# Attention into a two-layer MLP on one core: the first two attention units in steps of one pair of heads, and the first four MLP units over 512 tokens at once

## The chip, the core and the metric

The program runs on one core of a Trainium2 chip. The core has a matrix engine (TensorE, PE in the profile, with its weight loads as PEld), three engines for element-wise work (VectorE as DVE, ScalarE as ACT, GpSimd as POOL), and DMA queues that SyncE (SP) fills. The metric is the device time of one execution in microseconds; the median of the runs is quoted.

## What is computed

```python
# q, k, v: (2, 8, 768, 64);  x: (1536, 512);  d_ff = 2048, two MLP layers
k_sum = k.reshape(B, H, nb, 32, D).max(axis=3)       # 24 summary keys
v_sum = v.reshape(B, H, nb, 32, D).mean(axis=3)
scores_l = where(|i-j| < 16, q @ k.T / 8, -1e9)      # local window
scores_s = q @ k_sum.T / 8 + log(32)
a = softmax(concat(scores_l, scores_s))              # divided by sum + 1e-9
x = a @ concat(v, v_sum)
h = x @ moe_w_in                                     # layer 1
g = (a0 + a1*h + a2*h^2 + a3*h^3) / (1 + |b0||h| + |b1|h^2 + 1e-6)
x = g @ moe_w_out
h = x @ moe2_w_in;  out = (h * cos(h)) @ moe2_w_out  # layer 2
```

The weights arrive as 64-bit floats and are unpacked on the chip. Every MLP product is done in three matmuls on high and low parts (high by high, high by low, low by high), so that one MLP step has three matmuls where a plain one has one.

## The kernel before

Attention is cut into 12 units of 128 tokens with all 8 heads, which are held as 4 pairs (`NP`). A unit `u` goes through three functions. `attn_a` copies the keys of two windows of 96 tokens and the 24 summary keys into `kw`, makes 16 score matmuls into two PSUM tiles `sp`, then for each of its 8 (pair, head) slices one masked minimum on DVE (line 664) and one exponential on ACT (line 668), and at its end the normalisation (lines 672 to 683, the last step on POOL or DVE). `attn_b` transposes the normalised scores (8 matmuls into `ptp`, copies into `pt`). `attn_c` multiplies with the values (16 pairs of matmuls into `avp`) and stores the result as a high and a low part, `xH` and `xL`. Keys of the first batch are made by `k_pair`: one pair of heads at a time, in two DMAs, two groups of transposes (`ktp`), two copies and two maxima. `q_tile` transposes queries into `qT`; `v_mean0` makes the summary values.

The MLP is cut into units of one block `f` of 128 hidden features and one tile `T` of 512 tokens. `mlp_h` makes `h` from 12 matmuls, `ew1` works out the rational function on ACT, DVE and POOL (some ten instructions, then `split_g` into `gh` and `gl`), and `mlp_o` accumulates 12 matmuls into four PSUM tiles `acc`. `mlp_o` follows `mlp_h` three units later. `conv` unpacks the weights of one `f` (two matrices, each three DVE steps and a split into high and low). Only the first tile (layer 1, group 0, `T` 0) is cut in two halves of 256 tokens: line 992 gives it 8 units of 256 tokens, so the first four can begin when attention units 0 and 1 are done.

The order on every engine comes from a planner (class `Plan`). The functions above record operations with the engines that could run each one and an assumed cost; `fill` lists the attention steps, and the loop at lines 1080 to 1088 lays them between the MLP units so that an MLP unit comes after the attention units it needs (`pos_need`). The planner then works out latest times backwards from the end and places operations forwards by those times and by how soon an engine is free. Tile pools limit it: `ps` has four PSUM buffers that `sp`, `h` and some of the transposes share, `gh` and `gl` have three each, `raw` has three and the windows `kw` two. Each engine runs its list strictly in that order.

```python
992    subs = [(0, 256), (256, 256)] if (l, g, T) == (0, 0, 0) else [(0, TT)]
1046       pos_need.append(need[(TT * un.T + un.c + un.n) // 128 - 1])
```

Of the kernel before, what the change touches and what calls it, by code (L numbers as in the profile page):

```python
# [9 lines left out]
F32 = mybir.dt.float32  # L10
# [276 lines left out]
SPT = 1.2  # L287
# [3 lines left out]
def kernel(  # L291
# [322 lines left out]
    pr_t, pt_t = {}, {}  # L614
# [4 lines left out]
    def attn_a(u):  # L619
# [4 lines left out]
        sps = [psum([128, NP, KW], f"sp{hh}") for hh in range(2)]  # L624
        kks = {kr["k", i, y] for w in ws for i in range(w // 128, (w + WK - 1) // 128 + 1)
               for y in range(NP)}
        kw = kws[u % NKW]
        if t < NKW:
            P.op([("P", Shared(0.6)), ("A", act(192))], [kr[x] for x in kr.subs if x[0] == "s"], [kw["s"]],
                 lambda e: cp(e, kw.t[:, :, :, WK:KW],  # L630
                              ks().unsqueeze(2).to_broadcast([128, NP, 2, NB])))

        def windows(e):
            if ws[1] - ws[0] == 64:
                x = kk()[:, :, ws[0]:ws[0] + 128].rearrange("p n (a s) -> p n a s", a=2)
                x = bass.AP(x.tensor, x.offset, [x.ap[0], x.ap[1], x.ap[2], [1, WK]])
                cp(e, kw.t[:, :, :, 0:WK], x)
            else:
                for half in range(2):
                    cp(e, kw.t[:, :, half, 0:WK], kk()[:, :, ws[half]:ws[half] + WK])  # L640

        n = 768
        P.op([("P", Shared(1.2)), ("A", act(n)), ("V", dvef(n))], sorted(kks, key=id), [kw["w"]], windows)

        def mm(e):
            for pr in range(NP):
                for half in range(2):
                    for hh in range(2):
                        p0, c0 = 64 * hh, 64 * half
                        nc.tensor.matmul(out=sps[hh].t[c0:c0 + 64, pr, :],  # L650
                                         lhsT=qt.t[p0:p0 + 64, pr, c0:c0 + 64],
                                         rhs=kw.t[p0:p0 + 64, pr, half, :], start=True, stop=True)

        P.op([("T", SPT)], [qt, kw["s"], kw["w"]], sps, mm)
        su = new("sm", [128, 2, NP], F32, "su", 3)
        mn = new("sm", [128, 2, NP], F32, "mn", 3)
        m = masks[offs]
        scs = []
        for hh in range(2):
            sc = new("at", [128, NP, KW], F32, "sc", 4)  # L660
            sp = sps[hh]
            for pr in range(NP):
                P.op([("V", 0.19)], [sp], [sc[pr], mn[hh, pr]],
# [6 lines left out]
                         bias=mn.t[:, hh, pr:pr + 1], accum_out=su.t[:, hh, pr:pr + 1]))  # L670
            sus = [su[hh, pr] for pr in range(NP)]
# [12 lines left out]
            scs.append((sc, ss))  # L684
        pr_t[u] = scs
        P.now += SPT
# [324 lines left out]
    def add_a(u):  # L1011
        b, t = divmod(u, UPB)
        if u == 0:
            for i in range(NP):
                fill.append((k_pair, i, 30.0))
        elif t == 0:
            for i in range(6):
                fill.append((k_tile, i, LEADK))
        fill.append((q_tile, u, 30.0 if u < 2 else 8.0))
        fill.append((attn_a, u))  # L1020
        if t == 0:
            fill.append((v_mean1, LEADK) if b else (v_mean0, 24.0))
# [102 lines left out]
```

## Time and profile before

| | |
|---|---|
| median of 3 runs | 619.33 us (617.93 to 620.05) |
| profiled execution | 618.5 us, its span 616.8 us |
| PE busy | 595.5 us, 97% of the span |
| DVE, ACT, POOL busy | 477.8, 396.4, 413.7 us |
| granted clock of PE, mean | 0.994 |

The 618.5 us are the whole profiled execution, the span is the stretch from its first to its last instruction; 1.7 us lie outside it. A busy share of PE includes the drain of a matmul, so PE's rate is better read from the start of one matmul to the start of the next. The idle time of PE and what ended it is read from the list of waits, and its place in the program from the timeline.

### The profile page before, as it was taken

Reading aid. Unit: us, or ns where it says so; the run is one execution under the profiler, and the core shown is the slowest. Engines: PE = TensorE matmul, PEld = TensorE weight load, DVE = VectorE, ACT = ScalarE, POOL = GpSimd, SP = SyncE. Lnnn points to the kernel's source line nnn. Section 1 sums busy time; section 2 is a strip of 40 time slices with the busy share of each in tenths; the row PEclk is TensorE's granted clock in tenths of the full one; section 3 lists DMA queues with packets and bytes.
Section 4 is the critical chain, followed back from the end, with each engine's and each line's share of the span. In section 5 each row is a group of like instructions: output and inputs, shape, how many; then the busy total and the mean of one; then the engine's idle time right before and its main releaser. Section 6 shows DMA issues by size and latency. Waiting matters only on the chain.

```text
span 616.8 us, 9933 instructions
## 1 busy us (share of the span) xinstructions
PE 595.5 (97%) x3516; PEld 489.9 (79%) x3516; DVE 477.8 (77%) x919; ACT 396.4 (64%) x842; POOL 413.7 (67%) x409
## 2 busy tenths in 40 slices
PE   8778997999999999999999999999999999999997
PEld 7467876787888888888888878888888888888886
DVE  3999887758899989999999899569656875773541
ACT  5988799668767666786677656455455446544553
POOL 4487984657987878789868777568446754574332
PEclk9989999899999999999999999999999999999999
DMA  8986963100221222112122124213201330000112
GB/s 247 261 231 161 251 181 103 27 1 35 69 69 35 69 69 69 55 59 94 34 73 77 57 71 136 67 41 102 98 28 41 104 102 2 34 1 1 69 51 86
DMA packets 68714, 51.80 MB, mean 84 GB/s; under 512 B 37288, under 2 KB 62888, under 8 KB 68664
## 3 DMA queue, kind: packets, MB, share of 16 engines
q1 hardware_dynamic: 68376, 51.16, 28.0%
q8 instruction: 28, 0.46, 0.3%
q14 instruction: 22, 0.18, 0.1%
q10 hardware_dynamic: 288, 0.00, 0.0%
HBM read 47.71 MB, written 3.15 MB: 82 GB/s over the span
## 4 chain that ended last, share of the span: by engine, by line
PE 61%; DVE 20%; ACT 9%; POOL 4%; issue 3%; DMA 3%; SPq 0%; DVEq 0%; ACTq 0%; POOLq 0%
PE acc L943 29%; PE h L820 28%; ACT sc L668 2%; DVE te L868 2%; DVE tu L876 2%; DVE h L879 2%; DVE te L866 2%; DVE te L882 2%; DVE f L784 2%; DVE f L788 2%; DVE f L780 2%; ACT h L874 1%; PE avp L742 1%; POOL tu L864 1%; DMA big<-in_v_dram 1%
## 5 line engine op out<-in xcount | busy, mean ns | idle before, releaser
L820 PE MATMUL h<-xH,w 128*128 128x512 f32 (+1 forms) x544 | 172.8, 380 | 3.3 <-ACT pt L360 2.2
L839 POOL TENSOR_TENSOR gl<-te,gh 128x512 fp32r<-128x512 f32 (+1 forms) x100 | 135.0, 1350 | 7.4 <-ACT gh L360 0.9
L362 POOL TENSOR_SCALAR gh<-te 128x512 fp32r<-128x512 f32 (+1 forms) x84 | 59.3, 706 | 100.9 <-DVE te L906 80.9
L943 PE MATMUL acc<-gh,w 128*128 128x512 f32 (+1 forms) x416 | 123.5, 380 | 1.3 <-POOL gh L362 1.3
L820 PEld LDWEIGHTS h<-xH,w 128*128 128x128 f32 x544 | 100.9, 189 | 23.4 <-ACT pt L360 2.7
L943 PE MATMUL acc<-w,gh 128*128 128x512 f32 x384 | 118.4, 389 | 0.4 <-DVE xL L965 0.4
L820 PE MATMUL h<-xL,w 128*128 128x512 f32 (+1 forms) x272 | 103.0, 379 | 0.1
L898 DVE SCALAR_TENSOR_TENSOR h<-tu,h 128x512 f32<-128x512 int32 x96 | 66.4, 691 | 36.0 <-ACT te L360 34.9
L820 PE MATMUL h<-big,w 128*128 128x512 f32 x384 | 92.1, 389 | 0.9 <-DVE te L882 0.9
L943 PEld LDWEIGHTS acc<-gh,w 128*128 128x128 f32 x416 | 76.2, 190 | 16.6 <-POOL gh L362 1.5
L794 POOL TENSOR_TENSOR w<-f,w 128x512 fp32r<-128x512 f32 x62 | 84.2, 1360 | 6.2 <-ACT w L360 3.9
L820 PEld LDWEIGHTS h<-big,w 128*128 128x128 f32 x384 | 72.0, 188 | 16.3 <-DVE te L882 1.4
L943 PEld LDWEIGHTS acc<-w,gh 128*128 128x128 f32 x384 | 72.0, 188 | 15.8 <-DVE xL L965 0.9
L864 POOL TENSOR_TENSOR tu<-tu,tf 128x512 f32<-128x512 f32 (+1 forms) x52 | 67.1, 1291 | 19.6 <-ACT tf L856 19.5
L943 PE MATMUL acc<-gl,w 128*128 128x512 f32 (+1 forms) x208 | 78.3, 377 | 0.2 <-POOL gl L839 0.2
L943 PE MATMUL acc<-w,gl 128*128 128x512 f32 x192 | 74.7, 389 | 0.0
L901 ACT ACTIVATE h<-h 128x512 f32<-128x512 f32 x48 | 27.9, 582 | 60.4 <-DVE h L898 60.4
L906 DVE TENSOR_TENSOR te<-te,h 128x512 f32<-128x512 f32 x48 | 32.9, 685 | 35.1 <-ACT h L903 34.9
L820 PEld LDWEIGHTS h<-xL,w 128*128 128x128 f32 x272 | 51.3, 189 | 9.4 <-DVE xL L753 0.3
L893 ACT ACTIVATE tu<-h 128x512 int32<-128x512 f32 x48 | 28.7, 598 | 45.7 <-PE h L820 45.7
L784 DVE SCALAR_TENSOR_TENSOR f<-raw,f 128x512 int32<-128x512 int32 x64 | 56.1, 877 | 0.5
L788 DVE SCALAR_TENSOR_TENSOR f<-raw,f 128x512 int32<-128x512 int32 x64 | 56.0, 875 | 0.6
(100 smaller groups left out, 974.7 us busy)
## 6 DMA issues: line engine op xcount, KB each, us to landing
raw<-in_moe_w_in_dram SPq DMA_DIRECT2D x32, 512.0 KB, 3.7
raw<-in_moe_w_out_dram SPq DMA_DIRECT2D x32, 512.0 KB, 3.3
vw<-in_v_dram SPq DMA_DIRECT2D x24, 192.0 KB, 4.7
qk<-in_q_dram SPq DMA_DIRECT2D x10, 256.0 KB, 3.8
out_dram<-part SPq DMA_DIRECT2D x8, 256.0 KB, 2.0
part<-in_k_dram SPq DMA_DIRECT2D x8, 192.0 KB, 4.6
big<-in_v_dram SPq DMA_DIRECT2D x3, 512.0 KB
qk<-in_k_dram SPq DMA_DIRECT2D x6, 256.0 KB, 3.3
```

The lines of the kernel that those rows point to most:

```text
L362: nc.gpsimd.tensor_scalar(out=o, in0=i, scalar1=1.0, scalar2=1.0, op0=ALU.mult, op1=ALU.mult)
L784: lambda e, lohi=lohi, ft=ft: nc.vector.scalar_tensor_tensor(out=ft.t.bitcast(I32), in0=lohi()[1], scalar=-0x40000000, in1=ft.t.bitcast(I3 ...
L788: lambda e, lohi=lohi, ft=ft: nc.vector.scalar_tensor_tensor(out=ft.t.bitcast(I32), in0=lohi()[0], scalar=29, in1=ft.t.bitcast(I32), op0=A ...
L794: lambda e, ft=ft, w=w: E[e].tensor_tensor(out=w.t[:, 1, :], in0=ft.t, in1=w.t[:, 0, :].bitcast(F32), op=ALU.subtract),
L820: nc.tensor.matmul(out=h.t[:, 0:n], lhsT=lt, rhs=rt[:, kk, cs], start=(k0 == 0 and i == 0), stop=(k0 == 2 and i == 5))
L839: lambda e: E[e].tensor_tensor(out=un.gl.t[:, 0:n], in0=g.t[:, 0:n], in1=un.gh.t[:, 0:n].bitcast(F32), op=ALU.subtract))
L864: lambda e: E[e].tensor_tensor(out=U(), in0=U(), in1=Z(), op=ALU.add))
L893: lambda e: nc.scalar.activation(out=K().bitcast(I32), in_=H(), func=ACTF.Identity, scale=1.0 / (2.0 * math.pi)))
L898: lambda e, c=c: nc.vector.scalar_tensor_tensor(out=H(), in0=K().bitcast(I32), scalar=-c, in1=H(), op0=ALU.mult, op1=ALU.add))
L901: lambda e: nc.scalar.activation(out=H(), in_=H(), func=ACTF.Abs))
L906: lambda e: nc.vector.tensor_tensor(out=S_(), in0=S_(), in1=H(), op=ALU.mult))
L943: nc.tensor.matmul(out=dst, lhsT=lt, rhs=rt, start=(un.start and not have and i == 0), stop=(un.stop and i == 2), skip_group_check=have)
```

## The change

Two things change. First, `attn_a` takes a list of pairs of heads. Units 0 and 1 are now recorded one pair at a time: after `k_pair` of pair i come the windows, scores, minima and exponentials of that pair for unit 0 and for unit 1. The two `sp` tiles, `sc`, `su` and `mn` of a unit are allocated once and kept until its last pair, after which the new `soft_end` records the normalisation as before. The queries of units 0 and 1 move ahead of the keys of pairs 1 to 3. Second, the first tile is one piece of 512 tokens like all others, so its four MLP units wait for attention units 0 to 3, and `mlp_h`, `ew1` and `mlp_o` run 4 times with 512 columns where they ran 8 times with 256.

```diff
-    def attn_a(u):
+    def attn_a(u, parts=None):
...
-        sps = [psum([128, NP, KW], f"sp{hh}") for hh in range(2)]
...
+        if u not in sp_t:
+            sp_t[u] = ([psum([128, NP, KW], f"sp{hh}") for hh in range(2)],
+                       [new("at", [128, NP, KW], F32, "sc", 4) for hh in range(2)],
+                       new("sm", [128, 2, NP], F32, "su", 3), new("sm", [128, 2, NP], F32, "mn", 3))
+        sps, scs, su, mn = sp_t[u]
+        prs = range(NP) if parts is None else parts
...
         def mm(e):
-            for pr in range(NP):
+            for pr in prs:
...
-            for pr in range(NP):
-                P.op([("V", 0.19)], [sp], [sc[pr], mn[hh, pr]],
+            for pr in prs:
+                P.op([("V", 0.19)], [sp[pr]], [sc[pr], mn[hh, pr]],
...
+        if prs[-1] == NP - 1:
+            soft_end(u)
+
+    def soft_end(u):
+        sps, scs, su, mn = sp_t.pop(u)
...
-        subs = [(0, 256), (256, 256)] if (l, g, T) == (0, 0, 0) else [(0, TT)]
+        subs = [(0, TT)]
...
         if u == 0:
+            fill.append((k_pair, 0, 30.0))
+            fill.append((q_tile, 0, 30.0))
+            fill.append((q_tile, 1, 30.0))
             for i in range(NP):
-                fill.append((k_pair, i, 30.0))
-        elif t == 0:
+                if i:
+                    fill.append((k_pair, i, 30.0))
+                fill.append((attn_a, 0, (i,)))
+                fill.append((attn_a, 1, (i,)))
+            fill.append((v_mean0, 24.0))
+        if u < 2:
+            return
```

The planner lays out every engine anew. On ACT, at the start of the program, this stood before (`big` holds the transposed keys, the `sc,su<-sc,mn` rows are the exponentials):

```order
L360 COPY big<-ktp 128x384 x7
L360 COPY kw_104<-big 128x4x96 x2
L360 COPY big<-ktp 128x384
L360 COPY qT_106<-qtp 128x512
L360 COPY kw_104<-big 128x8x24
L360 COPY qT_107<-qtp 128x512
L360 COPY kw_105<-big 128x8x24
L360 COPY kw_104<-big 128x8x96
L668 ACTIVATE sc,su<-sc,mn 128x120 x9
```

All eight key copies stood ahead of the first exponential. In the changed kernel ACT begins with:

```order
L360 COPY big<-ktp 128x384
L360 COPY kw_104<-big 128x96 x2
L360 COPY big<-ktp 128x384
L360 COPY kw_104<-big 128x2x24
L360 COPY qT_106<-qtp 128x512
L360 COPY qT_107<-qtp 128x512
L360 COPY big<-ktp 128x384
L360 COPY kw_104<-big 128x96 x2
L675 ACTIVATE sc,su<-sc,mn 128x120
L360 COPY big<-ktp 128x384
L675 ACTIVATE sc,su<-sc,mn 128x120
```

The first exponential now stands behind three key copies, and the window and summary copies come in small pieces, one pair of heads each.

On PE, the first MLP matmul stood before right behind the scores of unit 3, with the values of units 0 and 1 done (`sp_571` is the last score tile of unit 3, `w_567` the output weights of the first `f`):

```order
L650 MATMUL sp_571<-kw_105,qT_107 64x120
L820 MATMUL h<-xH_112,w_464 128x256
L820 MATMUL h<-xL_113,w_464 128x256
...
L695 MATMUL ptp<-ident,sc 120x128 x4
L601 MATMUL qtp<-ident,qk 128x128 x4
...
L943 MATMUL acc_739<-gh,w_567 128x256 x2
L943 MATMUL acc_739<-gl,w_567 128x256
```

In the changed kernel it stands behind the values of unit 3 (`vw_111` belongs to unit 3, `w_656` and `w_781` are the two matrices of the first `f`, `w_841` the input weights of the second):

```order
L755 MATMUL avp<-pt,vw_111 64x64 x2
L513 MATMUL ktp<-ident,qk 128x128 x4
L833 MATMUL h<-xH_112,w_656 128x512
L833 MATMUL h<-xL_113,w_656 128x512
...
L708 MATMUL ptp<-ident,sc 120x128 x8
L513 MATMUL ktp<-ident,qk 128x128 x4
...
L833 MATMUL h<-xH_112,w_841 128x512
L513 MATMUL ktp<-ident,qk 128x128 x16
L956 MATMUL acc_981<-gh,w_781 128x512 x2
L956 MATMUL acc_981<-gl,w_781 128x512
```

Between the first `h` and the first accumulation PE now has one unit's transposes and values, the second `h` and 24 key transposes of the second batch.

On POOL, the stretch that ends in the first `gl` was before (`w_674` the second output matrix):

```order
L681 TENSOR_TENSOR sc<-sc,su 128x480
L864 TENSOR_TENSOR tu<-tu,tf 128x256
L362 TENSOR_SCALAR w_674<-f 128x512
L794 TENSOR_TENSOR w_674<-f,w_674 128x512
L864 TENSOR_TENSOR tu<-tu,tf 128x256
L362 TENSOR_SCALAR gh<-te 128x256
L839 TENSOR_TENSOR gl<-te,gh 128x256
```

and it is now:

```order
L696 TENSOR_TENSOR sc<-sc,su 128x480 x2
L362 TENSOR_SCALAR w_841<-f 128x512
L807 TENSOR_TENSOR w_841<-f,w_841 128x512
L877 TENSOR_TENSOR tu<-tu,tf 128x512
L362 TENSOR_SCALAR w_904<-f 128x512
L807 TENSOR_TENSOR w_904<-f,w_904 128x512
L362 TENSOR_SCALAR kw_104<-big 128x4x96 x2
L362 TENSOR_SCALAR kw_105<-big 128x8x96
L877 TENSOR_TENSOR tu<-tu,tf 128x512
L362 TENSOR_SCALAR gh<-te 128x512
L852 TENSOR_TENSOR gl<-te,gh 128x512
```

Three window copies have come between the first `tu` and the first `gh`, and each of the MLP's steps is twice as wide.

## Rows read from the trace of the kernel before

**Rows 1.** Busy time by stretch: span, then PE, PEld, DVE, ACT, POOL (us), granted clock.

```profile
7.10:31.10 24.00, 19.01 (x360) 13.83 (x355) 20.25 (x84) 22.04 (x76) 8.80 (x9) 1.00 1.01 282
31.10:39.70 8.60, 5.65 (x69) 4.64 (x65) 8.53 (x33) 8.26 (x30) 6.54 (x7) 1.00 1.05 267
39.70:60.00 20.30, 17.20 (x193) 15.68 (x194) 19.14 (x70) 16.69 (x58) 16.39 (x19) 0.92 0.66 182
60.00:131.60 71.60, 67.89 (x751) 54.50 (x749) 56.69 (x195) 58.90 (x177) 49.91 (x52) 0.98 0.47 122
131.60:600.00 468.40, 467.02 (x2060) 385.53 (x2057) 369.20 (x536) 282.62 (x491) 323.00 (x292) 1.00 0.19 59
```

**Rows 2.** Waits of PE over the whole span: us in total, times, longest.

```profile
PE h L820 <- ACT pt L360: 2.2, 2, 1.7
PE ptp L695 <- ACT pt L360: 2.0, 1, 2.0
```

**Rows 3.** Timeline of PE: start, us, instructions, idle time before and its releaser.

```profile
29.03 1.15 PE L742 MATMUL avp<-pt,vw 120*64 120x64 f32 x32
30.11 1.05 PE L650 MATMUL sp<-kw,qT 64*64 64x120 f32 x32
31.09 0.38 PE L820 MATMUL h<-xH,w 128*128 128x256 f32 x1
...
39.70 0.64 PE L943 MATMUL acc<-gh,w 128*128 128x256 f32 x2 [1.32 <-POOL gh L362]
...
99.02 1.03 PE L695 MATMUL ptp<-ident,sc 128*120 128x128 f32 x8
...
130.55 1.15 PE L742 MATMUL avp<-pt,vw 120*64 120x64 f32 x32
```

**Rows 4.** PE at 256 columns (timeline, matmuls 1 and 19 of a run).

```profile
32.05 0.28 PE L820 MATMUL h<-xL,w 128*128 128x256 f32 x1
...
34.21 0.28 PE L820 MATMUL h<-xL,w 128*128 128x256 f32 x1
```

**Rows 5.** PE at 512 columns, in the chain that ended last.

```profile
602.16 10.89 PE acc L943 x48
```

**Rows 6.** Timeline of ACT at the start.

```profile
7.14 1.79 ACT L360 COPY big<-ktp 128x384 f32<-128x384 f32 x4
...
15.84 0.39 ACT L668 ACTIVATE sc<-sc,mn 128x120 f32<-128x120 f32 x1 [0.33 <-DVE mn L664]
...
16.23 0.38 ACT L668 ACTIVATE sc<-sc,mn 128x120 f32<-128x120 f32 x1
...
16.61 0.38 ACT L668 ACTIVATE sc<-sc,mn 128x120 f32<-128x120 f32 x1
...
21.59 0.59 ACT L360 COPY pt<-ptp 120x512 f32<-120x512 f32 x1
22.07 0.40 ACT L668 ACTIVATE sc<-sc,mn 128x120 f32<-128x120 f32 x1
```

**Rows 7.** Groups up to 165 us: busy us, mean ns of one, idle before.

```profile
L360 ACT COPY kw<-big 128x192 f32<-128x192 f32 x3 | 1.1, 352 | 0.1
L854 ACT ACTIVATE tu<-h,co 128x512 f32<-128x512 f32 x13 | 8.9, 687 | 4.9 <-PE h L820 4.6 <-DVE h L879 0.2
L854 ACT ACTIVATE tu<-h,co 128x256 f32<-128x256 f32 x8 | 3.8, 473 | 2.7 <-PE h L820 2.6
L864 POOL TENSOR_TENSOR tu<-tu,tf 128x512 f32<-128x512 f32 x12 | 15.9, 1323 | 6.0 <-ACT tf L856 5.9
L794 POOL TENSOR_TENSOR w<-f,w 128x512 fp32r<-128x512 f32 x12 | 16.6, 1386 | 3.2 <-ACT w L360 2.6
L362 POOL TENSOR_SCALAR w<-f 128x512 fp32r<-128x512 f32 x8 | 5.3, 664 | 1.4 <-DVE f L788 1.3
```

**Rows 8.** Short stretches of PE alone: span, PE busy, granted clock.

```profile
40.00:42.00 2.00, 1.77 (x8) 0.50 0.54 211
...
108.00:110.00 2.00, 2.00 (x8) 0.54 0.00 0
```

More of the change, by code (lines that the diff above doesn't have):

```diff
@@ L627, in attn_a @@
+        sps, scs, su, mn = sp_t[u]
+        prs = range(NP) if parts is None else parts
+        p0, p1 = prs[0], prs[-1] + 1
+        n = p1 - p0
+        kks = {kr["k", i, y] for w in ws for i in range(w // 128, (w + WK - 1) // 128 + 1) for y in prs}
         kw = kws[u % NKW]
         if t < NKW:
-            P.op([("P", Shared(0.6)), ("A", act(192))], [kr[x] for x in kr.subs if x[0] == "s"], [kw["s"]],
-                 lambda e: cp(e, kw.t[:, :, :, WK:KW],
-                              ks().unsqueeze(2).to_broadcast([128, NP, 2, NB])))
+            sums = [kr[x] for x in list(kr.subs) if x[0] == "s" and x[1] in prs]
+            P.op([("P", pts(48 * n)), ("A", act(48 * n))], sums, [kw["s", y] for y in prs],
+                 lambda e: cp(e, kw.t[:, p0:p1, :, WK:KW],
+                              ks()[:, p0:p1].unsqueeze(2).to_broadcast([128, n, 2, NB])))
@@ L642, in attn_a @@
-        n = 768
-        P.op([("P", Shared(1.2)), ("A", act(n)), ("V", dvef(n))], sorted(kks, key=id), [kw["w"]], windows)
+                    cp(e, kw.t[:, p0:p1, half, 0:WK], kk()[:, p0:p1, ws[half]:ws[half] + WK])
+        c = 192 * n
+        P.op([("P", Shared(0.24 + 0.24 * n)), ("A", act(c)), ("V", dvef(c))], sorted(kks, key=id),
+             [kw["w", y] for y in prs], windows)
         def mm(e):
-            for pr in range(NP):
+            for pr in prs:
                 for half in range(2):
@@ L648, in mm @@
                     for hh in range(2):
-                        p0, c0 = 64 * hh, 64 * half
+                        r0, c0 = 64 * hh, 64 * half
                         nc.tensor.matmul(out=sps[hh].t[c0:c0 + 64, pr, :],
[L651 to L655, printed above, removed]
@@ L656, in attn_a @@
-        mn = new("sm", [128, 2, NP], F32, "mn", 3)
+                                         lhsT=qt.t[r0:r0 + 64, pr, c0:c0 + 64],
+                                         rhs=kw.t[r0:r0 + 64, pr, half, :], start=True, stop=True)
+        P.op([("T", SPT * n / NP)], [qt] + [kw[x, y] for x in "sw" for y in prs],
+             [sp[y] for sp in sps for y in prs], mm)
+        P.now += SPT * n / NP
         m = masks[offs]
-        scs = []
         for hh in range(2):
-            sc = new("at", [128, NP, KW], F32, "sc", 4)
-            sp = sps[hh]
-            for pr in range(NP):
-                P.op([("V", 0.19)], [sp], [sc[pr], mn[hh, pr]],
+            sc, sp = scs[hh], sps[hh]
+            for pr in prs:
+                P.op([("V", 0.19)], [sp[pr]], [sc[pr], mn[hh, pr]],
@@ L670, in attn_a @@
                          bias=mn.t[:, hh, pr:pr + 1], accum_out=su.t[:, hh, pr:pr + 1]))
+        if prs[-1] == NP - 1:
+            soft_end(u)
+    def soft_end(u):
+        sps, scs, su, mn = sp_t.pop(u)
+        pr_t[u] = []
+        for hh in range(2):
+            sc = scs[hh]
             sus = [su[hh, pr] for pr in range(NP)]
@@ L683, in attn_a @@
                      op=ALU.mult))
-            scs.append((sc, ss))
-        pr_t[u] = scs
-        P.now += SPT
+            pr_t[u].append((sc, ss))
     def attn_b(u):
```

14 lines of the change are left out of this document (6 added, 8 removed).

## The prediction

> **What bounds the kernel now.** I read the busy time by stretch first [rows 1]. From 131.6 us to 600 us PE is busy 467.02 of 468.40 us at full clock: there the kernel is a stream of matmuls at one per 10.89 / 48 = 0.227 us [rows 5], and nothing on another engine shows. Before that PE loses time while DVE and ACT are nearly full (from 7.1 to 31.1 us ACT is busy 22.04 of 24.00 us, and DVE 8.53 of 8.60 us in the next stretch). The first 7.1 us hold constants and the first key loads and stay as they are. So I count what PE loses from 7.1 us to the end of attention.
>
> The place to compare is the last value matmul of unit 11. Before, it starts at 130.55 us [rows 3] and is over at 131.6. Counting MLP matmuls ahead of it in PE's order gives before 96 + 96 of 256 columns and 60 + 36 of 512, so 192 in units of 512; in the changed kernel 108 + 84 = 192 of 512. Attention is the same too. PE has the same work ahead of that point and the same work behind it, and behind it nothing but PE counts. The change is worth the time by which this point moves.
>
> PE's loss up to it, before [rows 1]: idle 24.00 - 19.01 = 4.99, 8.60 - 5.65 = 2.95, 20.30 - 17.20 = 3.10 and 71.60 - 67.89 = 3.71, together 14.75 us. Half clock: a granted clock of 0.92 over 20.30 us is 3.2 us at 1.2 GHz, which cost half of that, 1.6; 0.98 over 71.60 us costs 1.4. Narrow matmuls: 18 of 256 columns take 34.21 - 32.05 = 2.16 us, 0.120 each [rows 4], against 0.227 / 2 = 0.1135; 192 of them lose 1.3 us. In all 19.0 us of 131.6.
>
> **The change part by part.**
>
> *The start.* The first exponential begins at 15.84 us [rows 6], behind all eight key copies. With pairs it stands behind three, so it can begin some 5 us earlier. But ACT was not idle in those 5 us: its idle time from 7.1 to 31.1 us is 1.96 us [rows 1]. Starting early brings work forward, it does not remove any, and the MLP now has to wait for four units. When does its first matmul run? The list on ACT from the first key copy to the cast of unit 3's values, with start-to-start times [rows 6]: 8 key copies at 1.79 / 4 = 0.45 are 3.6; 40 exponentials (units 0 to 3 and all of unit 4, which the planner puts in between) at 16.61 - 16.23 = 0.38 are 15.2; 16 copies and casts of 512 columns at 22.07 - 21.59 = 0.48 are 7.7. Copies of 192 columns take 0.352 [rows 7] less the overlap of 0.59 - 0.48 = 0.11, so 0.24: two make 0.5. The line through 192 and 512 columns gives 0.7 for one of 768 (an estimate). The 13 small window and summary pieces (8 of 96 columns, 5 of 48) are not in this trace: none is dearer than the 192-column copy, 3.1 together, none cheaper than the line's foot of 0.10, 1.2 together; the line gives 2.0, which I take. Two small sums 0.2. Total 29.9 us, from 7.14 to 37.0. With the 1.96 us that ACT waited before, and 0.7 us for the low part on DVE, the first `h` starts at 39.7 us (38 to 42), against 31.09 before [rows 3].
>
> PE's work ahead of it: before, 31.09 - 4.99 = 26.1 us. The order adds two score groups at 31.09 - 30.11 = 0.98, two value groups at 30.11 - 29.03 = 1.08, and 28 transposes at 1.03 / 8 = 0.13 [rows 3], 7.7 us. So PE has done 33.8 us of work at 39.7 us and lost 5.9 us. Before it had lost 4.99 + 2.95 = 7.9 us at the same moment. **Term 1: -2.0 us.**
>
> *The width.* 96 matmuls of 512 for 192 of 256. **Term 2: -1.3 us** by [rows 4, 5].
>
> *The new wait.* From the first `h` (call it 0) PE has in order: 12 matmuls 2.7, 12 transposes 1.6, values 1.1, the second `h` 2.7, 16 transposes 2.1: it reaches the first accumulation at 10.2. That needs `gh` and `gl`. `h` is done at 2.9; ACT has six exponentials ahead of `ew1`, so the two reads of `h` with one copy between end at about 4.5; POOL's sum takes 1.32 [rows 7], to 5.9. Then POOL has, ahead of `gh`, a weight split (0.66 + 1.39), three window copies (priced at 0.66 as the one-input step of [rows 7]; 2.0) and the sum of the second unit (1.32); `gh` 0.66 and `gl` 1.35 end at 11.9 and 13.3. The steps between on ACT and DVE, five at 0.5 to 0.7, end near 9.5 and are covered by POOL. PE waits 1.7, does two matmuls, waits 0.9. What queues behind: on PE the query transposes and scores of unit 6, on POOL the weight splits of the fourth block. The third accumulation meets the same queue: POOL has 17 us of listed work ahead of its `gl`, PE about 15, so another 2 us. Together 4.8 us; the bounds are nothing (PE's own list is long enough) and 5.8 (each POOL step end to end, without overlap). Before, the same stretch had 3.10 us of waits, 1.32 of them on `gh` [rows 1, 3]. **Term 3: +1.7 us.** Half clock after such a wait is counted as unchanged.
>
> *The relief on ACT.* One reading of `h` takes 473 ns at 256 and 687 at 512 columns [rows 7]: 2 x 473 - 687 - 110 of overlap is 0.15 us, with five such steps and four units 3.0 us. Against that the window and summary pieces cost 2.0 + 0.5 where two copies of 384 and two of 192 columns cost 1.2 by the line above, 1.3 more. Net 1.7 us off an engine that is 82% busy after 39.7 us and whose `pt` copies end 4.2 us of PE's waits [rows 1, 2]. It is worth between 0 and 1.7; I take half. **Term 4: -0.9 us.**
>
> *Nothing:* DMAs are the same transfers; the queries go ahead of six key loads, and the key loads are then later by two issues, hidden behind the first pair's copies. If that cover goes, each load costs PE part of a 0.45 us copy, inside the range of the first `h`.
>
> Sum: -2.0 - 1.3 + 1.7 - 0.9 = -2.5 us. The profiled execution of 618.5 us becomes 616.0. It lies 0.83 us under the median of the runs, 619.33; so the median should be **616.8 us**.
>
> **A rule that speaks against it.** After the waits between 31.1 and 39.7 us the clock is 0.50 in 40 to 42 us, and 0.54 in 108 to 110 us after a wait of 2.0 us [rows 2, 8]; yet from 7.1 to 31.1 us, with 4.99 us idle, it stays at 1.00 [rows 1]. The Trainium skill ("TensorE: Matmul & The Clock Gate", section "HAM oscillation — how this bites in real kernels") says that gaps of idleness throw the matrix engine back to its lower clock, so that the next burst starts cold. By that rule the longer attention-only phase could put the first `h` at half speed; the trace agrees for 40 us and not for the stretch ahead of 31.1. It is part of the slow rival below.
>
> **Rivals.**
>
> *More than forecast.* PE's list after the first `h` covers the chain, so neither the new waits nor the old ones of 39.7 to 60 us come, nor the half clock that followed: -2.0 - 1.3 - 3.1 - 1.6 - 0.9 = -8.9, 610.4 us. For it: 10 us of PE work stand between `h` and accumulation. Against: POOL's list is as long.
>
> *No change.* The pace up to 131.6 us is that of ACT and DVE, not of PE. ACT had done 22.04 + 8.26 = 30.3 us by 39.7 us before; by my list it has done 29.9 at that moment in the changed kernel. Then its remaining 75.6 us are only 1.7 shorter, PE fills the same holes, and a gain of 0.5 us is left: 618.8 us. For it: DVE and ACT at 82 to 99% until 60 us. Against: after 60 us both are near 80%.
>
> *Slower, POOL as the bound.* The eight normalisations of units 0 to 3 must now all come before the first MLP matmul, with weight splits between them, and then `gh` of units twice as wide. If the last normalisation ends so late that `h` starts after 42 us, term 1 is gone (+2.5), some 3 us of the first matmuls run at half clock (+1.5), and the third accumulation waits 2 us more: -2.5 + 2.5 + 1.5 + 2 = +3.5, 622.8 us. For it: POOL is 81% busy from 39.7 to 60 us. Against: before, it is idle more than half of 7.1 to 31.1 us.
>
> **How the numbers follow.** Forecast 0.36 (its own range 614.5 to 617.4), more than forecast 0.12, no change 0.27, slower 0.25. A difference under 0.3%, 1.9 us, cannot be told from none here. Faster 0.36 + 0.12 = 0.48, same 0.27, slower 0.25. The range reaches into both outer cases, 611.5 to 622.5 us.
>
> **What would show it.** Right: the first exponential near 11 us; the first `h` of 512 columns between 38 and 42 us; a wait of 1 to 3 us on POOL before the first accumulation; the last values over near 129 us; the rate behind it unchanged. Wrong: a first `h` after 42 us, a half clock at it, an accumulation that does not wait, or an idle PE behind the end of attention that was not there before.

## The result, and the profile after

The changed kernel takes 625.09 us (median of 4 runs, 624.20 to 627.30), the kernel before 619.06 us on the same chip: ratio 1.0096, 95% interval 1.0074 to 1.0118. It is 6 us slower; the forecast was 616.8 us and the range ended at 622.5.

| | before | after |
|---|---|---|
| profiled execution, its span | 618.5, 616.8 us | 624.2, 622.5 us |
| PE, DVE busy | 595.5, 477.8 us | 597.4, 481.4 us |
| ACT, POOL busy | 396.4, 413.7 us | 394.7, 414.5 us |
| last value matmuls begin | 130.55 us | 133.80 us |
| from there to the end of the span | 486.25 us | 488.70 us |

The last two lines split the 5.7 us by which the spans differ: 3.25 us lie ahead of the last value matmuls and 2.45 us behind them. By a count of its records PE has 2112 MLP matmuls of 512 columns left at that point in both kernels. The first part varies from execution to execution: in other runs below whose start is untouched, the last value matmuls begin at 131.39 us (kernel before) and at 134.01 to 134.32 us (changed kernel).

Busy time by stretch in the changed kernel, columns as in [rows 1]:

```profile
7.10:31.10 24.00, 21.40 (x378) 15.66 (x378) 15.77 (x87) 22.69 (x91) 10.04 (x15) 1.00 0.96 264
31.10:39.70 8.60, 5.68 (x114) 4.54 (x112) 8.60 (x37) 7.92 (x31) 5.43 (x6) 1.00 0.87 218
39.70:60.00 20.30, 15.99 (x138) 13.21 (x133) 20.12 (x49) 15.09 (x41) 16.95 (x17) 0.92 0.89 216
60.00:80.00 20.00, 14.59 (x117) 10.32 (x116) 19.65 (x46) 12.60 (x32) 16.57 (x15) 0.98 0.69 185
80.00:134.70 54.70, 53.28 (x542) 39.59 (x542) 37.57 (x138) 42.99 (x130) 36.54 (x35) 0.95 0.36 99
134.70:600.00 465.30, 462.33 (x2041) 380.71 (x2036) 373.02 (x535) 282.02 (x491) 317.97 (x286) 1.00 0.18 58
```

Read the third busy figure, DVE's: 8.60 of 8.60, 20.12 of 20.30 and 19.65 of 20.00 us, so from 31 to 80 us DVE hardly stops, while PE stands idle 4.31 and 5.41 us in the second and third of these stretches. From 7 to 31 us it is the other way round: DVE is idle 8.2 us where it was idle 3.75 before [rows 1]. The last row is new too: PE is idle 2.97 us there, 1.38 before (a matmul of 512 columns is recorded as some 0.39 us long, though PE starts one per 0.227 us [rows 5]; so busy includes the drain ahead of each wait, and idle time understates what a wait costs).

PE's longest waits after (us in total, times, longest), to be set against [rows 2]:

```profile
PE vmp L566 <- POOL raw L563: 4.5, 1, 4.5
PE ktp L513 <- DVE te L895: 2.5, 1, 2.5
PE h L833 <- DVE xL L766: 2.1, 2, 1.7
...
PE acc L956 <- ACT acc L360: 1.7, 2, 1.4
```

And where they stand, in PE's timeline (as [rows 3]):

```profile
43.23 0.50 PE L833 MATMUL h<-xH,w 128*128 128x512 f32 x1 [1.75 <-DVE xL L766]
...
55.37 1.97 PE L513 MATMUL ktp<-ident,qk 128*128 128x128 f32 x8 [2.49 <-DVE te L895]
56.99 1.20 PE L956 MATMUL acc<-gh,w 128*128 128x512 f32 x2
...
78.36 1.19 PE L566 MATMUL vmp<-raw,vsel 128*24 128x512 f32 x2 [4.50 <-POOL raw L563]
...
133.80 1.15 PE L755 MATMUL avp<-pt,vw 120*64 120x64 f32 x32
...
256.55 0.70 PE L956 MATMUL acc<-gh,w 128*128 128x512 f32 x2 [1.39 <-ACT acc L360]
...
258.06 0.73 PE L956 MATMUL acc<-gh,w 128*128 128x512 f32 x2 [0.56 <-DVE acc L365]
...
259.31 0.74 PE L956 MATMUL acc<-gh,w 128*128 128x512 f32 x2 [0.28 <-DVE acc L365]
```

The first `h` comes at 43.23 us and waits for DVE. The key transposes at 55.37 us wait for a DVE step of the MLP, the last polynomial step of the first unit (`te`): by the code `ktp` and `h` share the four PSUM buffers of `ps`, and this step is the last that reads the first `h`. The wait at 78.36 us is the mean of the second batch's values (`v_mean1`): its blocks are loaded into the three `raw` buffers that weight unpacking on DVE gives back, and added on POOL behind a weight cast that waits for DVE too. The last three rows are a hand-over of partial sums in layer 1: the four `acc` tiles are spilled and another tile's sums reloaded by copies on ACT and DVE (line 360, 365). Before, no hand-over held PE up in its records.

After the 4.50 us wait PE runs at half clock, as it did before after shorter ones [rows 8] (short stretches of the changed kernel, columns as in [rows 1]; the clock is the third number from the end, 0.50 to 0.52):

```profile
80.00:82.00 2.00, 1.43 (x4) 0.63 (x3) 0.61 (x1) 1.23 (x2) 2.00 (x2) 0.50 0.42 100
82.00:84.00 2.00, 2.00 (x5) 0.68 (x4) 1.52 (x3) 0.30 (x1) 1.63 (x3) 0.50 1.11 361
84.00:86.00 2.00, 2.00 (x4) 0.80 (x3) 0.00 (x0) 0.32 (x1) 2.00 (x3) 0.52 0.18 63
```

Why DVE is full: the weight-unpacking steps between 31 and 82 us, by group (busy us, mean ns of one), first before, then after:

```profile
L788 DVE SCALAR_TENSOR_TENSOR f<-raw,f 128x512 int32<-128x512 int32 x7 | 5.2, 737 | 0.0
L784 DVE SCALAR_TENSOR_TENSOR f<-raw,f 128x512 int32<-128x512 int32 x7 | 5.0, 718 | 0.0
L780 DVE TENSOR_SCALAR f<-raw 128x512 int32<-128x512 int32 x7 | 3.9, 552 | 0.0
```

```profile
L801 DVE SCALAR_TENSOR_TENSOR f<-raw,f 128x512 int32<-128x512 int32 x10 | 8.3, 830 | 0.0
L797 DVE SCALAR_TENSOR_TENSOR f<-raw,f 128x512 int32<-128x512 int32 x9 | 8.0, 889 | 0.1
L793 DVE TENSOR_SCALAR f<-raw 128x512 int32<-128x512 int32 x9 | 4.3, 483 | 0.0
```

21 steps and 14.1 us before, 28 steps and 20.6 us after. The two-input steps have become longer (0.73 to 0.86 us on average), and seven more steps fall into the full stretch, since unpacking starts at 28.44 us instead of 21.03 (by 82 us both kernels have started 30 such steps). Its first load stands later in SP's queue (before, after):

```profile
15.61 1.30 SPq L439 DMA_DIRECT2D raw<-in_moe_w_in_dram  x1
```

```profile
23.29 0.59 SPq L439 DMA_DIRECT2D raw<-in_moe_w_in_dram  x1
```

### The profile page after: what moved, and what is told of

The parts are those of the page before. It is cut to its first block, busy times and chain, and to the rows that moved or that the text cites. A ratio compares the mean times of both kernels' runs of the same rounds, so it can differ in the third digit from the quotient of the medians.

```text
span 622.5 us, 9723 instructions
## 1 busy us (share of the span) xinstructions
PE 597.4 (96%) x3420; PEld 484.0 (78%) x3420; DVE 481.4 (77%) x899; ACT 394.7 (63%) x830; POOL 414.5 (67%) x404
## 4 chain that ended last, share of the span: by engine, by line
PE 51%; DVE 32%; ACT 6%; issue 4%; POOL 4%; DMA 2%; SPq 0%; DVEq 0%; ACTq 0%; POOLq 0%
PE h L833 24%; PE acc L956 24%; DVE f L801 4%; DVE tu L889 4%; DVE f L797 3%; DVE te L895 3%; DVE h L892 3%; DVE te L879 3%; DVE te L881 3%; DVE f L793 3%; ACT h L887 2%; POOL tu L877 1%; DVE sc L671 1%; DMA part<-in_q_dram 1%; DVE acc L365 1%
## 5 line engine op out<-in xcount | busy, mean ns | idle before, releaser
L833 PE MATMUL h<-xH,w 128*128 128x512 f32 x512 | 170.2, 391 | 3.5 <-DVE xL L766 2.1
L852 POOL TENSOR_TENSOR gl<-te,gh 128x512 fp32r<-128x512 f32 x96 | 133.1, 1387 | 8.2 <-ACT gh L360 1.9
L956 PE MATMUL acc<-gh,w 128*128 128x512 f32 x384 | 122.3, 400 | 2.5 <-ACT acc L360 1.7
L362 POOL TENSOR_SCALAR gh<-te 128x512 fp32r<-128x512 f32 x78 | 56.4, 723 | 89.7 <-DVE te L919 80.7
L833 PEld LDWEIGHTS h<-xH,w 128*128 128x128 f32 x512 | 96.1, 188 | 24.9 <-DVE xL L766 2.6
L833 PE MATMUL h<-xL,w 128*128 128x512 f32 x256 | 99.7, 389 | 0.0
L956 PEld LDWEIGHTS acc<-gh,w 128*128 128x128 f32 x384 | 71.6, 191 | 21.0 <-issue 3.0
L877 POOL TENSOR_TENSOR tu<-tu,tf 128x512 f32<-128x512 f32 x48 | 66.9, 1394 | 26.1 <-ACT tf L869 26.0
L956 PE MATMUL acc<-gl,w 128*128 128x512 f32 x192 | 75.7, 395 | 0.6 <-POOL gl L852 0.6
L362 POOL TENSOR_SCALAR w<-f 128x512 fp32r<-128x512 f32 x46 | 30.9, 674 | 48.3 <-DVE f L801 30.2
```

The costliest lines, as they stand in the source:

```text
L362: nc.gpsimd.tensor_scalar(out=o, in0=i, scalar1=1.0, scalar2=1.0, op0=ALU.mult, op1=ALU.mult)
L833: nc.tensor.matmul(out=h.t[:, 0:n], lhsT=lt, rhs=rt[:, kk, cs], start=(k0 == 0 and i == 0), stop=(k0 == 2 and i == 5))
L852: lambda e: E[e].tensor_tensor(out=un.gl.t[:, 0:n], in0=g.t[:, 0:n], in1=un.gh.t[:, 0:n].bitcast(F32), op=ALU.subtract))
L877: lambda e: E[e].tensor_tensor(out=U(), in0=U(), in1=Z(), op=ALU.add))
L956: nc.tensor.matmul(out=dst, lhsT=lt, rhs=rt, start=(un.start and not have and i == 0), stop=(un.stop and i == 2), skip_group_check=have)
```

## Experiments

**Which part carries the loss.** The pairs with the first tile's halves put back, and the kernel before with the wide tile:

```diff
 e1 (after)   subs = [(0, 256), (256, 256)] if (l, g, T) == (0, 0, 0) else [(0, TT)]
 e2 (before)  subs = [(0, TT)]
```

> Units 0 and 1 by pairs of heads, but the first tile still in two halves of 256 tokens. Theory A (DVE is the bound from 31 to 80 us, because the unpacking of the first weights is pushed out of the idle time it had before 31 us, and four units of attention ahead of the MLP push it): the halves let the MLP start after unit 1, unpacking must come early again, so 617 to 620 us. Theory B (pairs are the cause: their small pieces on ACT and DVE and the queries ahead of the keys cost more than they bring): 623 to 626 us.

> The first tile over 512 tokens, attention as before. Theory A: the four units ahead of the MLP are the cause, so the loss is here too, 623 to 627 us, with the first matmul of 512 columns after 43 us and DVE busy over 95% from 35 to 80 us. Theory B (pairs are the cause): 617 to 620 us.

Pairs alone 620.01 us, ratio 1.0004 (0.9988 to 1.0021); width alone 624.14 us, 1.0086 (1.0055 to 1.0118). The width carries the loss, the pairs gain nothing. Both times fit theory A (pairs alone at its very edge), though the first matmul came at 41.00 us with the width alone, not after 43. "Nothing" for the pairs is a balance: their runs have a mean granted clock of 0.999 where those of the kernel before have 0.993, which by estimate is some 3.5 us of full clock won, and the time is the same. With the width PE's list shows the same first two waits:

```profile
PE vmp L566 <- POOL raw L563: 6.2, 1, 6.2
PE ktp L513 <- DVE te L882: 2.5, 1, 2.5
PE acc L943 <- ACT acc L360: 2.2, 2, 1.3
```

Its loss is not all at the start. Six more MLP matmuls (1.4 us) are left behind its last values than in the kernel before; counted at equal work, of the 5.0 us by which its span is longer 1.9 us lie ahead of that point and 3.1 us behind it.

**A column count between.** After, with the first tile in 128 and 384 columns (same line, `[(0, 128), (128, 384)]`).

> The changed kernel with the first four MLP units over 128 and 384 columns instead of all 512. Theory A (the width costs because the first matmul, and with it the chain over ACT, POOL and DVE, has to wait for all 512 columns of the layer's input: 43.2 us, where the halves began at 33.4 us with the pairs): the first matmul comes by 36 us, most of the loss at the start comes back, and the time is 620 to 622 us. Rival B (it costs because PE has fewer and larger pieces to fill its waits, or because the second, larger part is again late): the last value matmul comes 3 us or more later than with equal halves (126.9 us), 623 us or more.

631.37 us, ratio 1.0189 (1.0162 to 1.0215). The first `h` came at 32.45 us, 11 us earlier than in the changed kernel, and the time was 6 us worse: theory A's time is refuted, and an early first matmul did not bring the loss back here. The granted clock was 0.76 from 25 to 40 us and 0.79 from 40 to 55 us there (some 13.5 us at 1.2 GHz, 6.7 us lost), and the tile is cut into 96 matmuls more, so this run holds further losses that were not taken apart, and it does not say what an early first matmul is worth by itself.

**Is it DVE's work?** Two of the three unpack steps of the first eight matrices left out of the changed kernel, then the same of the kernel before.

```diff
+        left = {797: 8, 801: 8}          # lines of the steps; 784, 788 in the kernel before
+        for o in sorted(order, key=lambda o: o.seq):
+            n = o.fn.__code__.co_firstlineno
+            if left.get(n):
+                left[n] -= 1
+                o.fn = lambda e: None
```

> The changed kernel in its own order, with two of the three unpacking steps left out for the 8 matrices of the first four MLP blocks (the weights are then not the right numbers), 16 steps of 0.6 to 1.6 us on DVE. Theory A (DVE is the bound from 31 to 80 us): PE's waits between 40 and 82 us fall from 10 us to under 5, the first h starts before 42 us, and the time falls by 5 to 9 us, to 616 to 620 us. Theory C (PE's own list is too short while it waits for four units of attention, whatever DVE does): the first h stays near 43 us, the time falls by less than 2 us, 623 to 625 us.

> A control for the run that left unpack steps out of the changed kernel (622.3 us, 2.8 us less): the same two of three unpack steps of the first eight weight matrices left out of the kernel before, its order kept (these weights are then not those of the reference). Theory A (DVE bounds the start of the changed kernel, and bounds that of the kernel before by less, since there DVE begins to unpack 7 us earlier): 618.5 to 620 us, a gain under 1 us. Rival B (any kernel of this kind gains by less work on DVE, so the earlier run shows nothing of the change): 616 to 617.5 us, a gain of 2 us or more.

After: 622.33 us, ratio to the kernel before 1.0039 (1.0021 to 1.0057), where the changed kernel stands at 1.0096. Before: 619.14 us, 0.9993 (0.9977 to 1.0009), nothing. After, this falls between the two theories: the gain is 2.8 us and not 5 to 9, PE's idle time from 39.7 to 80 us is still 3.73 + 3.55 = 7.3 us (9.7 without the cut), and the first `h` comes at 41.64 us. In the kernel before, DVE's busy time from 39.7 to 60 us falls from 19.14 to 15.73 us without effect:

```profile
39.70:60.00 20.30, 18.70 (x219) 17.30 (x220) 15.73 (x65) 15.87 (x59) 14.04 (x18) 0.83 0.77 208
```

The clock in that row is 0.83, 0.92 without the cut [rows 1], so this one execution could hide a small gain; over all runs the mean granted clock is the same, 0.993 of 12 and 0.994 of 23. The traces place the gain of the changed kernel: its last values begin at 129.92 us, 3.88 us earlier and ahead of those of the kernel before, and from there to the end it takes 489.38 us, no less than without the cut (488.70):

```profile
129.92 1.15 PE L755 MATMUL avp<-pt,vw 120*64 120x64 f32 x32
```

So at the start DVE's unpacking holds the changed kernel up by as much as the change costs there, and it does not hold up the kernel before.

**The first weights earlier.** The first weight load ahead of unit 1's value loads, and its three unpack steps in DVE's early gap.

> The changed kernel in its own order but for four operations: the load of the first weight matrix goes ahead of the value loads of unit 1, and its three unpacking steps go into the 2.6 us that DVE waits before 24.8 us. Theory A: 2.5 us of DVE work leave the full stretch; 1.5 to 3 us less, 622 to 623.6 us. Theory D (the DMA queues are full up to 31 us, so whatever is loaded earlier makes another load later): no gain, 624.5 to 626 us, with the values of unit 1 later by about 2 us.

625.31 us, ratio 1.0093 (1.0059 to 1.0127): no gain. DVE was 2 us busier from 7 to 31 us (17.82), but PE waited 1.5 us for a key load and ran at half clock more often (granted 0.83, 0.91 and 0.83 in the three stretches of 20 us from 39.7 on). Its last values began at 135.33 us, 1.5 us later than in the changed kernel. Moving one of the matrices into the gap does not repay the gap; how much of that is the half clock was not taken apart.

**The longest wait.** The value blocks of `v_mean1` in tiles of their own (the early key rooms), with four steps moved in the order (two of them shown):

```diff
+            raw.make = lambda i=i: early[i // 2].t[:, 1024 * (i % 2):1024 * (i % 2) + 1024]...
...
+        ahead([by[426]], by[219])     # DVE: last polynomial step ahead of three unpack steps
+        ahead([by[430]], by[216])     # POOL: first addition ahead of a weight cast
```

> The changed kernel with one place of its order changed, around 70 to 85 us: the three second-batch value blocks are loaded into two idle 8 KB tiles (the early key rooms) instead of the three buffers that the weight unpacking shares, the first of the three additions on POOL stands ahead of a weight cast, and the last polynomial step of the unit whose g comes next stands ahead of three unpack steps on DVE, its low half on POOL ahead of that cast. Theory A (the 4.5 us wait before the value mean is the hold of the shared buffers and of POOL's order; PE would have had work): that wait falls below 2 us, the half-clock stretch at 79 us (6.8 us) becomes 3.4 us or goes, the last value matmul of the start comes 2 to 5 us earlier (near 131 us), and the time is 620 to 623 us. Rival B (DVE's full queue sets the pace of the start and the wait was only where it showed): the wait turns up again at the next accumulations, the last value matmul stays within 1 us of 134.7, and the time is 624 to 626 us.

623.85 us, ratio 1.0076 (1.0053 to 1.0100); the last value matmuls began at 133.15 us. The time lies between the two theories, the last values within 1 us of the changed kernel's, as rival B had it. The wait did not go; it split:

```profile
76.48 1.04 PE L568 MATMUL vmp<-part,vsel 128*24 128x512 f32 x2 [2.25 <-POOL part L565]
...
82.44 1.90 PE L568 MATMUL vmp<-part,vsel 128*24 128x512 f32 x2 [2.75 <-POOL part L565]
```

PE got its first block 2 us earlier and then waited 2.75 us for the second, behind POOL. That is close to rival B's mechanism, though the wait turned up at the next value block and not at the next accumulations. The half-clock stretch after it was shorter (3.4 us for 6.8). Of the 1.2 us gained only 0.65 lie ahead of the last values in the traces; the rest is not placed.

**The hand-over.** The copies that spill and reload partial sums stand in another order, ahead of other steps, about 250 to 258 us. The cut of the code is that of the mended form below:

```diff
+        order[i:i] = [by[x] for x in (1290, 1292, 1294, 1296, 1291, 1293, 1264, 1295)]
+        ahead([by[1297], by[1313]], by[1277])      # ACT: spill, reload
+        ahead([by[1319]], by[1278])                # ACT: reload
+        ahead([by[1315]], by[1266])                # DVE: reload ahead of a polynomial step
+        ahead([by[1317]], by[1213])                # DVE: reload ahead of an unpack step
```

> The changed kernel with the order changed at one hand-over of partial sums only (about 250 to 258 us): the four spills stand as early on ACT as their sums are done, the reloads behind them ahead of the next unit's two exponentials, the two reloads on DVE ahead of its unpack step. Start untouched. Theory A (the loss behind the last value matmul, 2.4 us, is the order in which ACT takes spills and reloads there): the three waits of PE at 256 to 259 us (1.4 + 0.6 + 0.3 us) go, and the time falls by 1.5 to 2.5 us, to 622.5 to 623.6. Rival B (ACT and DVE are behind there and something else is late in its place): waits of 1 us or more turn up on h or gl within the next 20 us, and the time falls by less than 0.8 us, 624.3 or more.

> Both edits together, the room and order at 70 to 85 us and the order at 250 to 258 us. If the two losses are separate, as I hold: the gains add up, to within 0.7 us of the sum of the two single runs; with theory A in both, 618 to 621 us, which is no faster than the kernel before by more than 0.3%. If the earlier end of the start moves the later collision elsewhere, the second gain is lost and the time is that of the first alone.

These two (626.38 and 624.96 us) tell nothing: two spills stood ahead of the accumulations that they copy, so a partial sum lacked a unit's share and PE waited for the spills. Mended:

> The hand-over at 250 to 258 us again, with each spill behind the accumulation that it copies (in the run before, two spills stood ahead of theirs, so PE had to wait for them and a partial sum lacked a unit). The changed kernel, nothing else touched: on ACT two spills fill the 1.6 us in which it waits for tu, the other two and the reloads stand ahead of the next unit's exponentials, on DVE the two reloads stand ahead of a polynomial step and an unpack step. Theory A (the loss behind the last value matmul is this order): the waits of PE at 256 to 259 us (1.4 + 0.6 + 0.3) go, from the last value matmul to the last matmul it takes 481.2 to 482 us instead of 483.6, and the ratio to the kernel before falls from 1.0096 to 1.006 to 1.007. Rival B (DVE and ACT are behind by then, whatever the order): as much wait turns up within the next 50 us, the stretch stays within 0.6 us of 483.6, and the ratio is 1.0085 or more.

> The mended hand-over once more, for its profile, since the first one was disturbed. With the rival that its time bore out (625.2 us, no gain): the waits at 256 to 259 us are smaller, and about as much waiting, 1.5 to 2.5 us, stands at other places up to 380 us. If the edit did nothing at all: the same waits at the same place.

625.25 us, ratio 1.0091 (1.0063 to 1.0118), and 625.12 us in one more execution, from which the rows are. The waits at 256 to 259 us are gone. They stand elsewhere, and from the last value matmul to the last matmul it takes 484.0 us, no less than 483.6:

```profile
279.24 0.70 PE L956 MATMUL acc<-gh,w 128*128 128x512 f32 x2 [1.74 <-DVE acc L365]
...
324.84 0.73 PE L956 MATMUL acc<-gh,w 128*128 128x512 f32 x2 [0.67 <-ACT acc L360]
...
328.22 0.73 PE L956 MATMUL acc<-gh,w 128*128 128x512 f32 x2 [0.37 <-ACT acc L360]
```

So the order at this place is not the cause by itself; other orders were not tried. The same kind of edit in the kernel with pairs and halves:

> The changed kernel's first two units by pairs of heads, the first four MLP units over two halves as before the change, and the order at the hand-over at 248 to 254 us changed in the same way as in the run above (spills early, reloads ahead of the next unit's steps). Without the last edit this kernel took 620.0 us against 619.8 for the kernel before. Theory A (its later loss, 1.9 us by the starts of the last value matmul and the last matmul, is the order at this hand-over, where PE waits 0.7 + 0.5 us): 618.3 to 619.3 us. Rival B (something else than the hand-over): 619.6 to 620.5 us.

620.05 us, ratio 1.0011 (0.9993 to 1.0030), no gain either: its wait of 0.54 us for DVE's reload at 254.72 us became one of 0.67 us at 274.65 us. No version here beats the kernel before with all of its work done.

**DVE's work ahead of the hand-over.** Two of three unpack steps of six later matrices left out (205 to 260 us), in the changed kernel, together with the early cut, and in the kernel before. The first cut of the code is the late cut in the changed kernel, the second comes from the run that was to make both cuts:

```diff
+        left = {1146, 1147, 1152, 1153, 1177, 1178, 1183, 1184, 1208, 1209, 1214, 1215}
+        for o in order:
+            if o.seq in left:
+                o.fn = lambda e: None
```

```diff
+        left = {797: 8, 801: 8}
...
+            if left.get(n) or o.seq in late:
+                left[n] = left.get(n, 0) - 1
+                o.fn = lambda e: None
```

> The changed kernel's order with two of the three unpack steps of six weight matrices left out on DVE, those of about 205 to 260 us (12 steps of about 0.7 to 1.4 us, so DVE has some 10 us less to do ahead of the hand-over; these weights are then not those of the reference). Order of all else kept. Theory B (DVE's backlog makes the hand-over late): the waits at 256 to 259 us and the one of about 1.2 us between 300 and 400 us shrink below 1 us in sum, the stretch from the last value matmul to the last matmul falls from 483.6 to below 482 us, ratio 1.006 to 1.007. Theory A (ACT's order of spills and reloads alone): the first wait, 1.4 us for ACT's reload, stays, and the stretch falls by less than 1 us.

> Both cuts of DVE's unpacking in the changed kernel, order kept: two of three steps of the first eight matrices (alone 2.8 us less) and of the six at 205 to 260 us (alone 3.6 us less); these weights are then not those of the reference. If both losses are work on DVE and separate, the gains add: 618 to 619.5 us, the kernel before within 0.3%, and from the last value matmuls to the end 485 to 486 us. Rival (an earlier end of the start only meets the hand-over earlier, so that one gain eats the other, or a third place loses it): 620.5 us or more.

> The control for the late cut: the same six matrices' two of three unpack steps left out of the kernel before, order kept (these weights are then not those of the reference). The trace of the kernel before shows no wait of PE at the hand-overs of this stretch, so with theory A (the late cut gained in the changed kernel what the change had cost there) this is no faster: within 1 us of the kernel before. Rival B (less work on DVE gains in any kernel of this kind): 2 us or more faster.

Late cut: 621.47 us, ratio 1.0036 (1.0020 to 1.0052), where the changed kernel stands at 1.0096. The kernel before with the late cut: 619.25 us, 0.9988 (0.9970 to 1.0006), nothing. In the changed kernel this cut took the waits at the hand-overs away: PE is busy for all of 200 to 260 us (57.76 of 60 without the cut). It gained more than theory B had said, and as with the early cut the traces say where (us):

| | last value matmuls begin | from there to the end of the span |
|---|---|---|
| before | 130.55 | 486.25 |
| before, early cut | 131.65 | 486.25 |
| before, late cut | 131.39 | 486.21 |
| changed | 133.80 | 488.70 |
| changed, early cut | 129.92 | 489.38 |
| changed, late cut | 134.01 | 485.29 |

```profile
134.01 1.15 PE L755 MATMUL avp<-pt,vw 120*64 120x64 f32 x32
```

In all six 2112 MLP matmuls are left behind that point. Each cut gains in its own stretch and in the changed kernel alone: 3.88 us at the start, 3.41 us behind it. An earlier end of the start does not heal the hand-over, so that loss is not DVE's backlog from the start carried on.

Whether the two gains add is not shown. The run that was to make both cuts took 618.05 us, ratio 0.9972 (0.9954 to 0.9990), but it leaves out far more: its counter falls below zero at the first late step and then counts as true, so that all later steps of the two lines go, 104 of the 128 two-input unpack steps instead of 28. The row of its trace behind attention has 87 DVE instructions and 71 us of DVE work less than that of the changed kernel:

```profile
134.70:600.00 465.30, 465.30 (x2079) 384.75 (x2079) 301.92 (x448) 285.28 (x496) 304.39 (x288) 1.00 0.18 58
```

With that PE has no idle time from the end of attention on. It bears out that DVE's work is what PE waits for there, but the hit on 618 to 619.5 us is luck: it comes from a larger cut, and no kernel before with the same cut stands beside it.

## Why the prediction was wrong, step by step

*Equal work on PE: right.* 2112 MLP matmuls are left behind the last values in both kernels, and 192 of 512 columns or their equal stand ahead.

*"Behind it nothing but PE counts": wrong, 2.45 us.* I took [rows 1], where PE is 99.7% busy from 131.6 us on, for proof that the other engines have slack there. DVE has little: 79% busy over the whole stretch (369.20 of 468.40 us), but from 200 to 300 us 93.1 of 100 us before and 93.7 after. Before, no hand-over was late; after, one was. Leaving out late DVE work returns this loss, and the one reordering tried moved it to the next hand-over. What the record does not show is why, with almost the same load on DVE, the new order is late: from 200 to 260 us DVE is busy 0.7 us more than before, ACT 2.9 us more and POOL 5.3 us less. An idle PE behind attention stood among my signs of being wrong, and so did a first `h` after 42 us; both came.

*Term 1, the start: right in its sum, wrong in its moment.* Up to 39.7 us PE had lost 2.60 + 2.92 = 5.52 us (5.9 predicted), and the first exponential came at 12.02 us (near 11). But the first `h` came at 43.23 us, outside 38 to 42. I built that moment from ACT's list and gave DVE 0.7 us for the low part; the wait in front of it, 1.75 us, ends with DVE's `xL`, which began at 42.51 us, 1 us after the high part was done, behind minima and an unpack step.

*Term 2, the width on PE: right.* Nine matmuls of the first `h` take 45.63 - 43.57 = 2.06 us from start to start, 0.229 each, where two of 256 columns take 0.240 [rows 4]: over 96 matmuls about 1.1 us for the 1.3 forecast.

*Term 3, +1.7 us: this step failed most.* Idle from 39.7 to 80 us is 4.31 + 5.41 = 9.7 us, where it was 3.10 + 0.41 = 3.5: +6.2 us. From 80 us to the end of attention PE made good 1.9 us of it (1.42 idle against 3.30). I had charged the chain with DVE's own steps, five of 0.5 to 0.7 us "covered by POOL", and not with what stands between them on DVE (unpack steps, maxima, minima), nor with PE's own list being held up by the buffer that the first `h` occupies: DVE's last step on it ended at 55.31 us, 12.1 us after the first `h`, and the first accumulation came 13.8 us after it where I had 11.9. The longest wait, 4.50 us for `v_mean1`, is in none of my terms. (My three waits also add up to 4.6 us and not 4.8, which changes little.) The wait on POOL before the first accumulation, 1 to 3 us in my list of signs, wasn't there at all: PE had been held up just before, at the key transposes, 2.49 us for DVE. So this term should have been +4.3 us where I had +1.7; 1.75 us of it are the wait in front of the first `h`.

*Half clock, "counted as unchanged": wrong.* By the granted clocks (0.92, 0.98 and 0.95 over 20.3, 20.0 and 54.7 us) some 9.5 us ran at 1.2 GHz and cost 4.8 us, against 1.6 + 1.4 = 3.0 before: +1.8. The profiled execution is a mild case: the mean granted clock is 0.988 over the four runs of the changed kernel and 0.993 to 0.994 over the runs of the kernel before, so by estimate (one minus the clock, times the span) some 7 us are lost to half clock against 4, about 3 of the 6 us. The Trainium skill has the rule that I had weighed, that gaps throw the matrix engine back ("TensorE: Matmul & The Clock Gate", "HAM oscillation — how this bites in real kernels"). It agrees with the half-clock stretches behind 55.37 and 78.36 us, though not with the first `h`: there the clock is 1.00 from 43.2 to 50 us, after an idle 1.75 us.

Sum of the start: -2.4 up to 39.7 us, +6.2, -1.9, +1.8 and -1.3 for the width give +2.4 us of the 3.25 measured; the rest is in the rounding of the clocks and in rows not taken apart. I had -2.5 us for it with term 4.

*"Nothing: DMAs are the same transfers": wrong.* They are the same, but SP issues the first weights 7.7 us later. I had looked at the key loads only. Moving one load back did not help, so that this made DVE late is argued from the order and not shown by a run.

*Term 4, the relief on ACT: right in size, no gain from it seen.* ACT's busy time fell 1.7 us, from 396.4 to 394.7, as worked out, though that sum also holds copies that the planner moved between engines, so the exact fit is luck. ACT is busy 12.60 of 20 us between 60 and 80 us: it was no longer the engine waited for.

*The rivals.* "Slower" had a first `h` after 42 us, half clock at it and late accumulations, and 622.8 us; it named POOL's normalisations. POOL is busy 5.43 of 8.60 us from 31.1 to 39.7 us, and what releases the first `h` is DVE: right side, wrong engine. I gave it 0.25 and set the end of the range by it; the time lies 2.3 us above its 622.8, about the 2.45 us behind attention that no rival had. "No change" fell with the time; of its reason, that ACT and DVE set the pace before, the control refutes the part on DVE, and the part on ACT has no run.

*How POOL comes in.* Two DVE steps and the POOL steps beside them, in the changed kernel:

```profile
63.42 1.64 DVE L797 SCALAR_TENSOR_TENSOR f<-raw,f 128x512 int32<-128x512 int32 x1
...
66.00 1.56 DVE L801 SCALAR_TENSOR_TENSOR f<-raw,f 128x512 int32<-128x512 int32 x1
```

```profile
63.19 1.32 POOL L807 TENSOR_TENSOR w<-f,w 128x512 fp32r<-128x512 f32 x1
...
65.72 1.29 POOL L852 TENSOR_TENSOR gl<-te,gh 128x512 fp32r<-128x512 f32 x1
```

Where POOL does nothing meanwhile, such a DVE step takes 0.68 us (mean of 34 in the changed kernel). Here each begins inside a POOL step and ends 0.55 us after it (65.06 behind 64.51, 67.56 behind 67.01). The Trainium skill says of a DVE step with two SBUF inputs that, against a POOL step that reads SBUF, it needs a shared port pair under an exclusive lock, and that the later of the two blocks altogether ("SBUF — State Buffer", "SBUF: two separate sides"). The rows agree. Between 31 and 82 us the 19 two-input steps took 16.3 us, 3.4 more than at 0.68 each; the 14 of before took 10.2, 0.7 more. So by estimate some 2.7 us of DVE's longer list are time spent beside POOL. No run here took this share away by itself.

*What stays open.* Why the planner's order for the wide tile leaves DVE idle 8.2 us early on: the four longest waits there are on ACT, PE and a weight load, and the one run that filled part of the gap gained nothing. Why the new order is late at the hand-over behind attention, where DVE has no more to do than before. Whether the two cuts add up. And which part of the 3.25 us would come back if only POOL's share went.

## What to carry to other kernels

A matrix engine that is 97% busy hides how little the next engine has in reserve: before merging units, add up the second-busiest engine's list in the stretch in question, with everything that stands between the steps of the chain, and look for idle time that it loses earlier and cannot get back. Where an engine was that full, moving a wait in the order moved it to the next place; a cut of that engine's work, with the same cut in the kernel before as control and the place of the gain read from the trace, told cause from coincidence. Count in the trace what a cut left out: here one left out 104 steps where 28 were meant. And the wider instructions saved about 1 us on PE, less than the waits that came with them.

## What was not expected of the hardware

The DVE steps of 0.68 us became 1.56 and 1.64 us beside POOL. And the half-clock stretches differ in length: 3.4 us after the wait of 2.49 us at 55.37 us, 6.8 us after the one of 4.50 us at 78.36 us, and none from 7 to 31 us, where PE was idle 2.60 us in small pieces. Why they differ was not tested.
